# Which queue issues the loads of x and of the softmax, and a planner that counts eight transfers in flight

## The chip, the core and the metric

The kernel runs on one core of a Trainium2 chip. The metric is the device time of one launch in microseconds (us). The core has five engines that run side by side: PE (matrix products), DVE (vector work), ACT (activations and copies), POOL and SP. In this kernel SP issues transfers and does nothing else; POOL issues transfers and does a few small steps at the start. A transfer that SP or POOL issues is moved by the core's 16 DMA engines, and what depends on it waits on a semaphore until it has landed.

## What is computed

Two stages follow each other, over a batch of 8 sequences of 4224 positions with 192 channels. The first is a dynamic convolution: for each position and each of 8 heads, 7 weights pass through a softmax and weigh the last 7 positions of x, 24 channels a head. The second takes that result: a depthwise convolution over 5 positions and a sigmoid make a gate, a matrix product makes a value, and the product of both passes through another matrix.

```python
w = exp(wg - max(wg)); w = w / (sum(w) + 1e-9)            # softmax over 7 taps, per head
y[s, h, :] = sum_k w[s, h, k] * x_pad[s + k, h, :]        # 24 channels a head
gate = sigmoid(sum_k conv_w[k] * y_pad[s + k])            # 5 taps, per channel
out = (gate * (y @ w_val)) @ w_out
```

## The kernel before

**Groups.** The positions are cut into 36 groups of up to 118, counted from 0. A group covers all 8 sequences. Its first step, the *bank*, forms the dynamic convolution as matrix products (L437): 128 small products, whose moving operand is `tb`, a banded matrix of softmax weights, and whose stationary operand is `xt`, a tile of x. So the bank of a group needs 8 loads of `tb` and 8 loads of `xt`. There are two buffers of `tb` and three of `xt`; a load may start once the bank that last used its buffer is done.

**After the bank.** ACT copies the result out of PSUM into `A`, `B` and a scratch `S` (L448, L451, L455). Eight small transfers from `S` fill the holes in `B` (four, L466) and `A` (four, L464); they are called *moves* below. Then come the first tap on ACT (L478), the other taps on DVE (L483), the sigmoid (L488), the value product on PE into `v` (L497 to L504), its product with the gate (L511, L513), the output product into `po` (L524, L531), its copy into `ot` (L546), and two stores of `ot` to the output (L555).

**Softmax.** The softmax of the weights runs ahead of the groups in ten parts (8, 8, 16, then 34 rows a partition, the last 28). A part is loaded into `wt` (L272), worked on by DVE and ACT, spread into `zt` by ACT (L320), and stored to a scratch `zd` in DRAM (L327), from where the loads of `tb` (L424) read it. A part of 34 rows feeds between four and five groups: 16 partitions of 34 rows a sequence are 544 positions.

**Who issues what.** SP issues the loads of `wt` and `tb`, the stores of the output, the first stores of `zd`, and the loads of x of the first and the last group. POOL issues the loads of x of the 34 groups between (L410, 272 transfers), the moves, and the later stores of `zd`. Each queue is served strictly in order: an instruction that waits holds all behind it.

**Eight semaphores a queue kind.** The framework gives the transfers of POOL eight completion semaphores in turn (`DMASW0` to `DMASW7` in the listings below), and those of SP eight others (`DMAHW0` to `DMAHW7`). Before a transfer is issued its engine waits until the last transfer with the same semaphore, the one eight ahead, has landed.

**What sets the order.** A planner, `Order.run`, plays through the whole program with estimated durations. At each step it takes, of the operations whose inputs are ready, the one that can start first on its engine, and breaks near ties by a due time (`key`, in units of groups). The order in which it picks them is the order in which the instructions stand on each engine. It believes that a transfer lands `bytes / RATE` plus `LAND` after the ones before it, with 260 GB/s and 2.8 us for SP and 3.8 us for POOL. It doesn't know of the eight semaphores.

Of the kernel before, what the change touches and what calls it, by code (L numbers as in the profile page):

```python
# [16 lines left out]
class Order:  # L17
# [4 lines left out]
    SWITCH = 0.1  # L22
    SEM = 0.08
    RATE = 260e3
    LAND = {"SP": 2.8, "ACT": 2.8, "POOL": 3.8}

    class Op:
# [14 lines left out]
    def run(self):  # L42
        for o in self.ops:
            o.left = len(o.deps) + len(o.behind)
            for d in o.deps:
                d.users.append((o, True))
            for d in o.behind:
                d.users.append((o, False))
        free, mode, dma = {}, {}, 0.0
        open_ = {}  # L50
        for n, o in enumerate(self.ops):
            if not o.left:
                open_.setdefault(o.eng, []).append((n, o))
        number = {id(o): n for n, o in enumerate(self.ops)}
        done = 0
        while done < len(self.ops):
            best = None
            for eng, c in open_.items():
                if not c:
                    continue  # L60
                t = free.get(eng, 0.0)
                first = min(max(t, o.ready) for _, o in c)
                n, o = min(((n, o) for n, o in c if max(t, o.ready) <= first + self.SLACK), key=lambda x: (x[1].key, x[0]))
                s = max(t, o.ready)
                if best is None or s < best[0]:
                    best = (s, n, o)
            s, n, o = best
            open_[o.eng].remove((n, o))
            e = s + o.dur
            if o.mode is not None:  # L70
                if mode.get(o.eng, o.mode[0]) != o.mode[0]:
                    e += self.SWITCH
                mode[o.eng] = o.mode[-1]
            free[o.eng] = e
            o.start, o.end = s, e + self.SEM
            if o.bytes:
                dma = max(dma, e + 0.8) + o.bytes / self.RATE
                o.end = dma + self.LAND[o.eng]
            o.fn()
            done += 1  # L80
            for u, lands in o.users:
                u.left -= 1
                u.ready = max(u.ready, o.end + u.delay if lands else e)
                if not u.left:
                    open_.setdefault(u.eng, []).append((number[id(u)], u))
        return max(o.end for o in self.ops)
# [3 lines left out]
def tile_dynconv_gated_moe(  # L90
# [9 lines left out]
    nc = tc.nc  # L100

    B, S, D = x.shape
# [3 lines left out]
    P = 128  # L106
# [64 lines left out]
    add = od.add  # L171
# [74 lines left out]
    class Softmax:  # L246
# [34 lines left out]
        def max(self, k):  # L281
            a, b = self.cut[k]
            nc.vector.tensor_reduce(out=self.mx[:, a:b], in_=self.wt[:, a:b], axis=AX.X, op=ALU.max)
# [45 lines left out]
    soft = []  # L329
    zstore = []  # L330

    def softmax(r0, R, k0, k1, early, k2, behind=()):

        s = Softmax(r0, R)
        old = soft[-2]["last"] if len(soft) > 1 else []
        n = s.n * ROW
        b0 = add("DVE", 0.06, early - 1e-3, s.begin, old, behind=behind)
        ld = [add("SP", 0.6, early, lambda: s.load(nc.sync), [b0], bytes=P * n * 4)]
        h = len(s.cut)
        steps = 5 * h + 1 + len(s.zc)  # L340
        done = [0]
# [38 lines left out]
    class Group:  # L380
# [23 lines left out]
        def load_x(self, j):  # L404

            r0 = self.s - FRONT
            if self.whole():
                src = bass.AP(tensor=x.tensor, offset=x.offset + (j * S + r0) * D,
                              ap=[[D, G], [G * D, NGR], [1, D]])
                nc.gpsimd.dma_start(out=self.xb[:, j, 0:D], in_=src)  # L410
            else:
                lo, hi, p = self.rows(j)
                src = bass.AP(tensor=x.tensor, offset=x.offset + (r0 + G * j + lo) * D,
# [180 lines left out]
    for name, cs, w, key in (("c", slice(2 * D, NWT), "DVE", -30), ("v", slice(0, D), "POOL", -29),  # L594
                             ("o", slice(D, 2 * D), "POOL", 1.0)):
        a = lw
# [32 lines left out]
    for m, gp in enumerate(gr):  # L629
        if 2 <= m < len(PARTS) - 1:  # L630
# [4 lines left out]

        old = T[m - 3]["bank"] if m >= 3 else [*xpad, xz]
        late = (() if m == 0 else T[m - 1]["loadt"]) if m < 3 else ()
        d["loadx"] = [add("POOL" if gp.whole() else "SP", 0.55, (-90, -35, -1)[m] if m < 3 else m - 2.2,
                          lambda gp=gp, j=j: gp.load_x(j), old, bytes=G * B * D * 4, behind=late)
                      for j in (range(B) if gp.whole() else gp.chunks)]  # L640
        use = [o for a, sts in rows if a < gp.s + n for o in sts] + [front]
# [86 lines left out]
```

## Time and profile before

| | |
|---|---|
| median of 3 runs | 588.81 us (587.95 to 588.96) |
| the profiled execution | 587.95 us, of which the profile's span is 586.2 us |
| mean granted clock of PE | 0.932 |
| PE busy | 484.9 us, 83% of the span |
| DVE busy | 438.5 us, 75% |
| ACT busy | 345.0 us, 59% |
| POOL busy | 330.2 us, 56% |
| moved by the DMA engines | 123.17 MB, 210 GB/s over the span |

POOL's busy time holds its transfer issues, each about half a microsecond; SP's issues count as no engine's busy time, and its view is a list of issues in order of time. The gap between the median and the span, 2.6 us, lies outside what the profile covers or is scatter between runs.

### The profile page before, as it was taken

To read this page: it belongs to the slowest core of one execution; us is meant where nothing else is said; L and a number is where in the kernel's file an instruction comes from. 1 tells how busy PE (TensorE), PEld (TensorE's weight loads), DVE (VectorE), ACT (ScalarE), POOL (GpSimd) and SP (SyncE) were. 2 spreads that over 40 slices of the span, in tenths; PEclk is the share of its full clock that TensorE was granted. 3 is DMA by queue.
4 is the path that set the end of the run, shared out by engine and by line. 5 is a ranking of instruction groups with operands and counts; after the bars stand their busy time and mean duration, and the time that the engine had idled before them with its cause. 6 is when DMAs were issued, how large, how long until landed. Compare 5 with 4: busy or idle time off the path is not lost.

```text
span 586.2 us, 15839 instructions
## 1 busy us (share of the span) xinstructions
PE 484.9 (83%) x6278; PEld 327.0 (56%) x6278; DVE 438.5 (75%) x488; ACT 345.0 (59%) x533; POOL 330.2 (56%) x613
## 2 busy tenths in 40 slices
PE   2033868599848988999979997998999999999994
PEld 1033535386525764566746673765766675767653
DVE  6776396679857299898887889878975679667780
ACT  4435554478535667458666766586585656546641
POOL 9535956256470666657457455677576687522410
PEclk7557879799987999999979998999999999999999
DMA  5989689738799998879997989799789868775222
GB/s 156 213 239 242 144 223 257 200 99 236 216 236 228 283 266 243 207 207 246 290 259 187 267 217 275 212 261 252 194 217 259 248 158 200 205 183 164 66 60 89
DMA packets 105869, 123.17 MB, mean 210 GB/s; under 512 B 17938, under 2 KB 95615, under 8 KB 103107
## 3 DMA queue, kind: packets, MB, share of 16 engines
q1 hardware_dynamic: 79779, 65.40, 42.5%
q0 software_dynamic: 26016, 56.75, 36.1%
q8 instruction: 50, 0.82, 0.6%
q14 instruction: 24, 0.20, 0.1%
HBM read 64.55 MB, written 51.43 MB: 198 GB/s over the span
## 4 chain that ended last, share of the span: by engine, by line
PE 40%; DMA 30%; POOL 13%; issue 8%; ACT 4%; DVE 2%; SPq 1%; POOLq 0%; ACTq 0%; DVEq 0%
DMA zd<-zt 13%; PE po L524 10%; PE pa L437 10%; POOL xt L410 7%; DMA A<-S 6%; PE po L531 5%; DMA xt<-in_x_dram 5%; PE v L501 5%; DMA tb<-zd 3%; PE v L499 3%; PE v L504 3%; PE v L497 3%; POOL A L464 2%; DMA raw_c<-cd 1%; POOL B L466 1%
## 5 line engine op out<-in xcount | busy, mean ns | idle before, releaser
L483 DVE SCALAR_TENSOR_TENSOR aA<-A,wf,aA 128x944 f32<-128x944 f32 (+1 forms) x144 | 171.6, 1192 | 26.6 <-ACT aA L478 22.8
L437 PE MATMUL pa<-tb,xt 128*32 128x122 f32 (+1 forms) x4608 | 140.5, 276 | 48.8 <-DMA tb<-zd 43.1
L410 POOL DMA_DIRECT2D xt<-in_x_dram x272 | 143.8, 549 | 44.0 <-DMA A<-S 8.7
L437 PEld LDWEIGHTS pa<-tb,xt 128*32 128x32 f32 x4608 | 127.7, 110 | 64.0 <-issue 56.1
L483 DVE SCALAR_TENSOR_TENSOR aB<-B,wf,aB 128x472 f32<-128x472 f32 (+1 forms) x144 | 101.2, 703 | 46.2 <-ACT aB L478 39.0
L466 POOL DMA_DIRECT2D B<-S x144 | 74.7, 525 | 95.8 <-ACT B L451 83.5
L524 PE MATMUL po<-wf,aA 128*118 128x192 f32 (+1 forms) x576 | 117.2, 349 | 11.8 <-DVE aA L511 9.4
L524 PEld LDWEIGHTS po<-wf,aA 128*118 128x118 f32 (+1 forms) x576 | 94.6, 188 | 43.2 <-issue 20.1
L464 POOL DMA_DIRECT2D A<-S x144 | 74.2, 521 | 69.2 <-DMA zd<-zt 36.9
L546 ACT COPY ot<-po 118x768 f32<-118x768 f32 (+1 forms) x72 | 57.8, 803 | 82.3 <-PE po L531 49.4
L531 PE MATMUL po<-wf,aB 64*118 64x192 f32 (+1 forms) x576 | 68.6, 358 | 26.6 <-ACT ot L546 16.8
L531 PEld LDWEIGHTS po<-wf,aB 64*118 64x118 f32 (+1 forms) x576 | 45.8, 183 | 42.6 <-ACT ot L546 18.9
L501 PE MATMUL v<-A,wva 128*128 128x472 f32 (+1 forms) x144 | 63.6, 562 | 0.0
L455 ACT COPY S<-pa 64x488 f32<-64x488 f32 (+1 forms) x72 | 40.5, 562 | 31.1 <-PE pa L437 30.6
L488 ACT ACTIVATE aA<-aA 128x944 f32<-128x944 f32 (+1 forms) x36 | 35.5, 986 | 32.5 <-DVE aA L483 32.5
L511 DVE TENSOR_TENSOR aA<-v,aA 128x944 f32<-128x944 f32 (+1 forms) x36 | 40.7, 1130 | 13.7 <-PE v L504 8.1
L320 ACT COPY zt<-wt 128x192 f32<-128x192 f32 (+3 forms) x100 | 39.1, 461 | 17.5 <-DVE wt L308 11.4
L478 ACT ACTIVATE aA<-A,wf 128x944 f32<-128x944 f32 (+1 forms) x36 | 38.9, 1081 | 14.2 <-DMA A<-S 14.2
L501 PEld LDWEIGHTS v<-A,wva 128*128 128x128 f32 x144 | 27.7, 192 | 31.0 <-issue 30.4
L448 ACT COPY A<-pa 128x488 f32<-128x488 f32 (+1 forms) x72 | 40.5, 565 | 6.5 <-PE pa L437 5.3
L497 PE MATMUL v<-A,wvm 128*64 128x472 f32 (+1 forms) x144 | 38.0, 605 | 7.1 <-DMA A<-S 5.2
L499 PE MATMUL v<-B,wvd 128*128 128x472 f32 (+1 forms) x72 | 39.3, 627 | 0.0
(60 smaller groups left out, 367.5 us busy)
## 6 DMA issues: line engine op xcount, KB each, us to landing
xt<-in_x_dram POOLq DMA_DIRECT2D x272, 96.0 KB, 4.2
tb<-zd SPq DMA_DIRECT2D x285, 88.0 KB
out_dram<-ot SPq DMA_DIRECT2D x35, 672.0 KB
zd<-zt POOLq DMA_DIRECT2D x14, 1104.0 KB, 8.1
wt<-in_weight_gen_dram SPq DMA_DIRECT2D x6, 1120.0 KB
zd<-zt POOLq DMA_DIRECT2D x6, 920.0 KB, 7.5
A<-S POOLq DMA_DIRECT2D x140, 30.5 KB, 4.4
B<-S POOLq DMA_DIRECT2D x140, 15.2 KB, 4.8
```

The source lines that it names most:

```text
L410: nc.gpsimd.dma_start(out=self.xb[:, j, 0:D], in_=src)
L437: nc.tensor.matmul(out=pa[Q * c:Q * c + Q, w * j:w * j + w], lhsT=self.xb[:, u * HB + j, C * h:C * h + Q], rhs=self.t[:, u * HB + j, PAD / ...
L464: nc.gpsimd.dma_start(out=self.A[q:q + n], in_=self.S[p:p + n])
L466: nc.gpsimd.dma_start(out=self.B[HD * u + q:HD * u + q + n], in_=self.S[p:p + n, w * u:w * u + w])
L483: nc.vector.scalar_tensor_tensor(out=a, in0=self.part(g, j), scalar=cw[:, g, j:j + 1], in1=a, op0=ALU.mult, op1=ALU.add)
L497: nc.tensor.matmul(out=v2[HD * u:HD * u + HD, 0:n], lhsT=wvm, rhs=A[u], start=True, stop=False, tile_position=(0, HD * u))
L499: nc.tensor.matmul(out=v2[:, 0:n], lhsT=wvd, rhs=Bt, start=False, stop=True)
L501: nc.tensor.matmul(out=v01[:, u, 0:n], lhsT=wva, rhs=A[u], start=True, stop=False)
L511: nc.vector.tensor_tensor(out=a, in0=self.v01[:, :, 0:n], in1=a, op=ALU.mult)
L524: nc.tensor.matmul(out=po[0:n, u, D * t:D * t + D], lhsT=self.aA[:, c:c + n], rhs=woa, start=first and t == 0, stop=not first, skip_group_ ...
L531: nc.tensor.matmul(out=po[0:n, u, D * t:D * t + D], lhsT=self.aB[hs, c:c + n], rhs=wob[hs], start=first and t == 0, stop=not first, skip_g ...
L546: nc.scalar.copy(out=self.ot[0:n, :, 2 * k:2 * k + 2, :].rearrange("p u t d -> p u (t d)"), in_=self.po[0:n, :, 0:2 * D])
```

## The change

Three things change. The loads of x of the 34 middle groups are issued by SP instead of POOL, and the planner's price for one such issue goes from 0.55 to 0.5 us. The loads of `wt` of the softmax's parts from the fifth on are issued by POOL instead of SP (six parts, eight transfers, since the last part has three). And the planner now knows the eight semaphores: it keeps a list of landing times for POOL and one shared by SP and ACT, and an operation that moves bytes can't start before the one eight ahead on its list has landed, by the planner's own estimate.

```diff
+    LANES = 8
     LAND = {"SP": 2.8, "ACT": 2.8, "POOL": 3.8}
...
         free, mode, dma = {}, {}, 0.0
+        lanes = {"SP": [], "POOL": []}
+        lanes["ACT"] = lanes["SP"]
+
+        def lane(o):
+
+            c = lanes[o.eng] if o.bytes else ()
+            return c[-self.LANES] if len(c) >= self.LANES else 0.0
+
...
-                first = min(max(t, o.ready) for _, o in c)
-                n, o = min(((n, o) for n, o in c if max(t, o.ready) <= first + self.SLACK), key=lambda x: (x[1].key, x[0]))
-                s = max(t, o.ready)
+                at = [(max(t, o.ready, lane(o)), n, o) for n, o in c]
+                first = min(a[0] for a in at)
+                s, n, o = min((a for a in at if a[0] <= first + self.SLACK), key=lambda x: (x[2].key, x[1]))
...
                 o.end = dma + self.LAND[o.eng]
+                lanes[o.eng].append(o.end)
...
-        ld = [add("SP", 0.6, early, lambda: s.load(nc.sync), [b0], bytes=P * n * 4)]
+        q = QUEUES[0 if len(soft) < 4 else 2]
+        ld = [add(q[0], 0.6, early, lambda e=q[1]: s.load(e), [b0], bytes=P * n * 4)]
...
-                nc.gpsimd.dma_start(out=self.xb[:, j, 0:D], in_=src)
+                nc.sync.dma_start(out=self.xb[:, j, 0:D], in_=src)
...
-        d["loadx"] = [add("POOL" if gp.whole() else "SP", 0.55, (-90, -35, -1)[m] if m < 3 else m - 2.2,
+        d["loadx"] = [add("SP", 0.5, (-90, -35, -1)[m] if m < 3 else m - 2.2,
```

Since the planner's rules and prices change, the order changes on every engine. The lists below name, for each instruction, its line, its operation, what it writes and reads, and the shape; the lines of the changed program are about ten higher for the same statement.

POOL, early in the program, before: two stores of `zd`, the moves of group 2, and the loads of x that stand around them. The semaphores that each waits for are in brackets.

```order
L410 DMA xt1_81<-in_x_dram 128x1x192 [waits DMASW4_49,PE_49]
L327 DMA zd_79<-zt0_77 16x8x2208 [waits DMASW5_49,Activation_49]
L327 DMA zd_79<-zt1_78 16x8x2208 [waits DMASW6_49,Activation_49]
L466 DMA B_571<-S_548 8x488 [waits DMASW7_49,Activation_49]
L466 DMA B_571<-S_548 8x488 [waits DMASW0_49]
L466 DMA B_571<-S_548 8x488 [waits DMASW1_49]
L466 DMA B_571<-S_548 8x488 [waits DMASW2_49]
L464 DMA A_592<-S_548 8x976 [waits DMASW3_49,Activation_49]
L464 DMA A_592<-S_548 8x976 [waits DMASW4_49]
L464 DMA A_592<-S_548 8x976 [waits DMASW5_49]
L464 DMA A_592<-S_548 8x976 [waits DMASW6_49]
L410 DMA xt2_82<-in_x_dram 128x1x192 [waits DMASW7_49,PE_49]
```

The same place in the changed program: the stores of the same softmax part and the moves of groups 1 and 2.

```order
L337 DMA zd_79<-zt0_77 16x8x2208 [waits DMASW2_49,Activation_49]
L475 DMA A_446<-S_427 8x976 [waits DMASW3_49,Activation_49]
L475 DMA A_446<-S_427 8x976 [waits DMASW4_49]
L475 DMA A_446<-S_427 8x976 [waits DMASW5_49]
L475 DMA A_446<-S_427 8x976 [waits DMASW6_49]
L337 DMA zd_79<-zt1_78 16x8x2208 [waits DMASW7_49,Activation_49]
L337 DMA zd_79<-zt0_77 16x8x1840 [waits DMASW0_49,Activation_49]
L477 DMA B_611<-S_598 8x488 [waits DMASW1_49,Activation_49]
L477 DMA B_611<-S_598 8x488 [waits DMASW2_49]
L477 DMA B_611<-S_598 8x488 [waits DMASW3_49]
```

Before, the third and the fourth move into `A` wait on `DMASW5` and `DMASW6`, the semaphores of the two stores that stand just ahead of the same group's moves. Now no load of x stands between, one store stands between the moves of group 1, and the semaphore of a store comes up again among the moves of the next group.

SP, some groups later, before: loads of `tb` and stores of the output, without x.

```order
L424 DMA tb_75<-zd 16x8x176 x8
L424 DMA tb_76<-zd 16x8x176 x4
L555 DMA out_dram<-ot 112x8x192
L555 DMA out_dram<-ot 6x8x192
L424 DMA tb_76<-zd 16x8x176 x4
L272 DMA wt<-in_weight_gen_dram 128x1x2240
L424 DMA tb_75<-zd 16x8x176 x3
```

SP, the changed program in its regular stretch.

```order
L435 DMA tb_75<-zd 16x8x176 x8
L421 DMA xt_82<-in_x_dram 128x1x192 x8
L566 DMA out_dram<-ot 112x8x192
L566 DMA out_dram<-ot 6x8x192
L435 DMA tb_76<-zd 16x8x176 x8
L421 DMA xt_80<-in_x_dram 128x1x192 x8
L566 DMA out_dram<-ot 112x8x192
L566 DMA out_dram<-ot 6x8x192
```

A group now has 18 transfers on SP where it had ten, and the loads of the next group's x stand between the loads of this group's `tb` and the stores.

SP at the start of the changed program: the loads of `tb` for group 0, the x of group 1, and then its `tb`.

```order
L435 DMA tb_75<-zd 16x8x176 x6
L282 DMA wt<-in_weight_gen_dram 128x1x2240
L337 DMA zd<-zt_78 16x8x1472
L435 DMA tb_75<-zd 16x8x176
L421 DMA xt_81<-in_x_dram 128x1x192 x8
L435 DMA tb_76<-zd 16x8x176
```

Before, those eight loads of x stood on POOL, on a queue of their own beside SP's loads of `tb`; now SP issues them after the last `tb` of group 0.

## The prediction

> **What bounds the kernel now.** I first cut the span into five stretches with the view of busy time by window (after each engine's busy time comes the number of instructions, then the granted clock, the share of the 16 DMA engines and the rate), then took the same view of the bank's line alone.
>
> ```profile
> core 0: us, PE busy (x) PEld busy (x) DVE busy (x) ACT busy (x) POOL busy (x), PEclk, DMA share, GB/s
> 0.00:60.00 60.00, 14.30 (x270) 11.71 (x270) 41.83 (x56) 27.69 (x50) 36.21 (x55) 0.66 0.86 212
> 60.00:160.00 100.00, 80.45 (x1024) 53.82 (x1025) 75.14 (x83) 60.45 (x92) 56.20 (x104) 0.91 0.73 195
> 160.00:400.00 240.00, 214.40 (x2782) 143.56 (x2780) 191.10 (x207) 154.77 (x238) 145.65 (x280) 0.96 0.90 243
> 400.00:560.00 160.00, 158.12 (x2104) 106.76 (x2105) 119.96 (x133) 94.54 (x147) 92.11 (x177) 1.00 0.73 191
> ...
> 60.00:160.00 100.00, 23.03 (x768) 20.85 (x768) 0.91 0.73 195
> 160.00:400.00 240.00, 62.24 (x2048) 55.91 (x2048) 0.96 0.90 243
> 400.00:560.00 160.00, 44.98 (x1536) 41.09 (x1536) 1.00 0.73 191
> ```
>
> A bank has 128 products, so the three long stretches hold 6, 16 and 12 banks: 16.7, 15.0 and 13.3 us a group. PE stands idle for 45.7 us of the first stretch, 19.6 of the second, 25.6 of the third and 1.9 of the fourth. The fourth is bound by PE. Two banks there show the pace when nothing is waited for:
>
> ```profile
> 435.20 3.75 PE L437 MATMUL pa<-tb,xt 128*32 128x122 f32 x128
> 448.06 3.75 PE L437 MATMUL pa<-tb,xt 128*32 128x122 f32 x128
> ```
>
> That is 12.9 us a group. The other stretches are held up by something else. The chain that ended last names it, over the whole span:
>
> ```profile
> PE 40%; DMA 30%; POOL 13%; issue 8%; ACT 4%; DVE 2%; SPq 1%; POOLq 0%; ACTq 0%; DVEq 0%
> ```
>
> Transfers and POOL together are 43% of the chain. POOL's list in order of time shows how, at the place that the first two listings of the change stand for:
>
> ```profile
> 71.75 4.22 POOL L410 DMA_DIRECT2D xt<-in_x_dram  x8
> 76.39 1.08 POOL L327 DMA_DIRECT2D zd<-zt  x2 [0.42 <-DMA xt<-in_x_dram]
> 77.49 2.08 POOL L466 DMA_DIRECT2D B<-S  x4
> 79.56 1.03 POOL L464 DMA_DIRECT2D A<-S  x2
> 83.59 0.52 POOL L464 DMA_DIRECT2D A<-S  x1 [3.00 <-DMA zd<-zt]
> 89.02 0.52 POOL L464 DMA_DIRECT2D A<-S  x1 [4.91 <-DMA zd<-zt]
> ```
>
> The last two moves of group 2 have their data, but wait until the two stores eight ahead have landed. The chain of waits runs through it: the store, the move, then the first tap that needs `A`.
>
> ```profile
> 76.93 11.81 DMA zd<-zt
> 88.74 0.28 issue
> 89.02 6.28 DMA A<-S
> 95.32 0.04 ACTq L478
> 95.36 0.05 issue
> 95.40 1.09 ACT aA L478
> ```
>
> In the third stretch the waits of POOL's moves into `A` are these (us in total, times, longest):
>
> ```profile
> POOL A L464 <- DMA zd<-zt: 21.3, 8, 7.4
> POOL A L464 <- DMA xt<-in_x_dram: 10.0, 6, 3.7
> POOL A L464 <- DMA B<-S: 7.8, 2, 5.0
> ```
>
> **The change, part by part.** *POOL's queue.* It loses 272 issues, and gains eight.
>
> ```profile
> L410 POOL DMA_DIRECT2D xt<-in_x_dram x272 | 143.8, 549 | 44.0 <-DMA A<-S 8.7
> xt<-in_x_dram POOLq DMA_DIRECT2D x272, 96.0 KB, 4.2
> zd<-zt POOLq DMA_DIRECT2D x14, 1104.0 KB, 8.1
> ```
>
> Eight loads of x are 4.4 us of issue a group; the eight softmax loads, at the 549 ns of such an issue, are 4.4 us in all. What matters more is the count: with only eight moves a group, a store of `zd` has until the next group's moves to land, and 8.1 us is shorter than the 12.9 of a group. At 76 us the fourth move would go right behind the first two, at 79.56 + 1.03 + 0.52 = 81.1 instead of 89.02: 7.9 us. The same happens at 147 us:
>
> ```profile
> 147.25 1.09 POOL L327 DMA_DIRECT2D zd<-zt  x2 [3.82 <-issue]
> 154.52 0.52 POOL L464 DMA_DIRECT2D A<-S  x1 [3.02 <-DMA zd<-zt]
> 159.21 0.52 POOL L464 DMA_DIRECT2D A<-S  x1 [4.16 <-DMA B<-S]
> ```
>
> with 3.0 + 4.2 = 7.2 us. Both are 15.1 of the 19.6 us that PE is idle in that stretch. What is late next is DVE, 75.1 busy of 100, and SP's longer list. The gain lies between 0 (the banks wait for SP instead) and 15.1; I take 9, nearer the waits that are seen, since the DMA engines have room there (share 0.73).
>
> In the third stretch PE's idle 25.6 us is less than the 39.1 that the moves wait, so part of that was covered. The floor is set elsewhere: 0.90 of 240 us is 216 us of work for the DMA engines, against 16 x 12.9 = 206 for PE and 191 for DVE. So the gain can't pass 24 us while the bytes cost what they do. The fullest 40 us show how near the engines come:
>
> ```profile
> 160.00:200.00 40.00, 29.39 (x357) 20.33 (x356) 22.02 (x24) 20.22 (x35) 19.78 (x39) 0.87 0.94 251
> ```
>
> At 0.94 the work takes 216 / 0.94 = 230 us: 10 us gained. I take that, with 0 and 24 as ends.
>
> *The price of the bytes on the other queue.*
>
> ```profile
> q1 hardware_dynamic: 79779, 65.40, 42.5%
> q0 software_dynamic: 26016, 56.75, 36.1%
> ```
>
> SP's queue (q1) moves 65.40 / 42.5 = 1.54 MB for each percent of the engines' span, POOL's 56.75 / 36.1 = 1.57. The x (272 x 96 KB = 26.7 MB) costs 17.4% there instead of 17.0%, 2 us over the kernel, 1 us in the third stretch, which leaves 9 of the 10.
>
> The Trainium skill says in "DMA: Bandwidth & Descriptors", section "Issuing engines are not separate DMA queues", that transfers run on the same 16 engines whoever issues them, and that a second issuer saves only the sequencer's time. The two rates agree with that within 2%; taken alone it gives the second rival below.
>
> *SP's queue.* It gets eight more a group. A quiet group and a crowded one:
>
> ```profile
> 506.72 5.04 SPq L424 DMA_DIRECT2D tb<-zd  x8
> 511.86 1.03 SPq L555 DMA_DIRECT2D out_dram<-ot  x2
> 522.93 4.46 SPq L415 DMA_DIRECT2D xt<-in_x_dram  x7
> ...
> 269.32 4.16 SPq L424 DMA_DIRECT2D tb<-zd  x3
> 273.57 1.25 SPq L555 DMA_DIRECT2D out_dram<-ot  x2
> 274.87 4.27 SPq L424 DMA_DIRECT2D tb<-zd  x5
> ```
>
> Quiet, 18 transfers take 5.04 + 8 x 0.64 + 1.03 = 11.2 us, under the 12.9 of PE. Crowded, the ten took 9.7 instead of 6.1, 3.6 us more: SP itself is held while earlier transfers drain. If that surplus stays per group, 18 take 14.8; if it grows with the count, 18 x 0.97 = 17.5, over the 15.0 that a group takes now. Behind a late SP stand the next loads of `tb`, and then the bank. I take the first, which costs nothing against 15.0 but leaves no room; in the fourth stretch, where 11.2 stands against 12.9 and a surplus may appear, I take 2 us of loss for its 12 groups, between 0 and 12 x (14.8 - 13.3) = 18.
>
> *The start.* PE's first bank waits for `tb`:
>
> ```profile
> PE pa L437 <- DMA tb<-zd: 43.1, 3, 33.6
> 20.00:40.00 20.00, 1.29 (x28) 1.32 (x32) 15.64 (x30) 4.85 (x13) 7.65 (x10) 0.50 0.92 219
> ```
>
> The engines are nearly full there (0.92), and x of group 1, 8 x 96 KB = 786 KB, now goes behind the `tb` of group 0: 786 / 219 = 3.6 us earlier for the first bank. Group 1 needs both and gains less. I take 2, between 0 and 3.6.
>
> *The order as such.* Every engine's list is redrawn, with the same work on it. A misplaced instruction costs a single wait of the kind that the view of waits has as its longest; for PE on ACT this is 7.8:
>
> ```profile
> PE po L531 <- ACT ot L546: 16.8, 6, 7.8
> ```
>
> I take 0, with 8 us either way.
>
> The sum: 2 + 9 + 9 - 2 = 18 us gained. The profiled execution took 587.95 us (span 586.2 and 1.75 around it), which gives 570; the median of the runs is 0.9 higher, so the forecast is **571 us**.
>
> **The rivals.** *SP becomes the bound (slower).* If the surplus grows part of the way with the count, a group of the third stretch takes SP midway between 14.8 and 17.5, 16.2 us: 16 x (16.2 - 15.0) = 19 us lost there, 12 x 0.5 = 6 in the fourth, against 2 + 9 gained before: 14 us lost, 603. It decides from a mean issue of 15.0 / 18 = 0.83 us on; the quiet rows give 0.62, the crowded ones 0.97. Against it: when SP is slow the engines have less to drain, and the surplus shrinks. The Trainium skill ("DMA: Bandwidth & Descriptors", "Queues, rings and completion order") has each DMA engine take the queues in turn, packet by packet. The rows of the two queues give mean packets of 2.2 KB on POOL's and 0.8 KB on SP's, so by that rule SP's loads of `tb` and x would come off worse while a store of `zd` or a load of `wt` is under way, which speaks for this rival.
>
> *The bytes are the bound anyway (no change).* The third stretch is at 0.90; POOL's waits on landings would be the engines' queue seen from the issuer, and the freed issues would only wait elsewhere. Then the third stretch gains nothing, and what the second gains is bytes moved early, given back in the third: 589 less 0 to 2, 588. Against it: in the second stretch the share is only 0.73.
>
> *The waits were nearly all (faster than forecast).* Both ends are reached: 3.6 + 15.1 + 24 = 43, 546 us.
>
> *The planner still believes too much (half the gain).* The rule of eight now matches what the listings show each transfer waiting for, but the planner prices a load of x on SP at 0.5 us, where SP took this for the loads of x that it already issues (min, median, max in ns):
>
> ```profile
> L415 SPq DMA_DIRECT2D xt<-in_x_dram x15: 563/598/876, 3.6 to 526.8; - x15
> ```
>
> By its prices (0.65 for `tb`, 0.5 for x, 0.55 for a store) a group's 18 take 10.3 us, not 11.2 to 14.8. What depends on them then stands too early in the lists and waits, and half of the 18 remains: 580.
>
> **Chances.** Forecast 0.40, the half gain 0.15, the large gain 0.13, the bytes 0.09, SP as the bound 0.23. The likeliest one's own range is 560 to 580. The range must leave out no more than 0.2: I let go most of the large gain's far end and the upper half of SP's case, and keep the rest: **551 to 600**. A measurement of this kernel tells about 0.2% (1.2 us) from no change. Faster has the first three and 0.02 of the bytes' case, 0.70; the same 0.06; slower 0.24.
>
> **What would show it.** Right: no wait of a move on a store of `zd` or on x over a few us; the third stretch at 14.4 us a group with the DMA share at 0.93 or more; the chain with less POOL and more PE; SP's issues at a mean under 0.8 us; the first bank at 35 to 37 us. Wrong: banks that wait on `tb` or xt after the start, SP's issues of `tb` and x stretched beyond 0.83 us, or the fourth stretch slower than 13.3 us a group, all three of SP's case; a third stretch still at 15.0 us with POOL's waits gone, of the bytes'.

## The result, and the profile after

The changed kernel takes 613.11 us (median of 4, 611.97 to 614.59) against 588.38 us (587.70 to 588.96) for the kernel before on the same chip: a ratio of 1.042 (95% interval 1.040 to 1.045). It is 25 us slower, where 18 us of gain had been predicted. Times in this document are medians of all executions of a kernel, while ratios leave out an execution that took over 1.5% longer than the fastest of the same kernel, so the two need not divide out exactly.

The stretches of the changed kernel, in the view by window, for all engines and below for the bank's line alone (now L448):

```profile
0.00:60.00 60.00, 18.75 (x250) 13.35 (x250) 44.07 (x62) 30.32 (x51) 34.42 (x46) 0.66 0.85 210
60.00:160.00 100.00, 79.01 (x1057) 54.39 (x1057) 82.51 (x86) 63.00 (x94) 27.18 (x54) 0.91 0.80 222
160.00:400.00 240.00, 195.97 (x2378) 131.25 (x2380) 177.14 (x190) 135.86 (x218) 65.39 (x130) 0.92 0.80 223
400.00:560.00 160.00, 157.20 (x2162) 107.67 (x2152) 109.04 (x120) 90.88 (x138) 51.76 (x104) 1.00 0.71 188
...
60.00:160.00 100.00, 25.02 (x800) 22.96 (x800) 0.91 0.80 222
160.00:400.00 240.00, 53.70 (x1740) 49.24 (x1744) 0.92 0.80 223
400.00:560.00 160.00, 47.41 (x1599) 42.86 (x1588) 1.00 0.71 188
```

With 128 products a bank these are 6.25, 13.6 and 12.5 banks: 16.0, 17.6 and 12.8 us a group, where it was 16.7, 15.0 and 13.3. The second and the fourth stretch are better than before. The whole loss is in the third, and there the DMA engines have fallen from 0.90 to 0.80: they are not what is short.

The chain's shares after:

```profile
PE 60%; DMA 10%; ACT 8%; DVE 7%; SPq 7%; issue 5%; POOL 2%; ACTq 0%; DVEq 0%; POOLq 0%
```

Transfers and POOL have gone from 43% to 12%. POOL now has time to spare, as its longest entry in the view of waits shows (total, times, longest): the moves wait for their data, and stores of `zd` or loads of x no longer hold them.

```profile
POOL B L477 <- ACT B L462: 304.9, 36, 20.7
```

SP, at two places of its timeline in the changed kernel, one while stores of `zd` and loads of `wt` are under way on POOL's queue, one in the fourth stretch:

```profile
106.00 5.67 SPq L435 DMA_DIRECT2D tb<-zd  x7
111.71 11.36 SPq L421 DMA_DIRECT2D xt<-in_x_dram  x8
123.17 7.03 SPq L566 DMA_DIRECT2D out_dram<-ot  x2
...
412.35 5.10 SPq L421 DMA_DIRECT2D xt<-in_x_dram  x8
417.54 3.27 SPq L435 DMA_DIRECT2D tb<-zd  x4
```

The same eight loads of x take 11.36 us at the one place and 5.10 at the other, both issued without a pause. This reading suggested SP as the cause, but it is only a part of the story.

A finer cut says where the time went. I took the start of the first, the ninth, the seventeenth and the last bank from the timeline's rows of the bank's line. The last two columns are not measurements: they are the times at which the planner (`Order.run`) itself believes that these banks start, read from its list.

| us between starts of banks | before | after | planned, before | planned, after |
|---|---|---|---|---|
| span's start to bank 0 | 38.7 | 35.4 | 36 | 37 |
| bank 0 to 8 | 150.4 | 130.7 | 123 | 128 |
| bank 8 to 16 | 102.3 | 158.8 | 103 | 155 |
| bank 16 to 35 | 260.8 | 252.1 | 248 | 250 |
| planner's total | | | 548 | 608 |

At bank 8 the changed kernel is 23 us ahead (3.3 + 19.7). In the next eight groups it loses 56.5, and it wins 8.7 back in the rest. The planner had planned that loss: 155 us instead of 103 for these eight groups.

### The profile page after: what moved, and what is told of

Its sections match the earlier page's. It is cut to its first block, busy times and chain, and to the rows that moved or that the text cites. A ratio compares the mean times of both kernels' runs of the same rounds, so it can differ in the third digit from the quotient of the medians.

```text
span 611.0 us, 15563 instructions
## 1 busy us (share of the span) xinstructions
PE 493.4 (81%) x6278; PEld 334.7 (55%) x6278; DVE 441.6 (72%) x488; ACT 341.7 (56%) x531; POOL 186.7 (31%) x349
## 4 chain that ended last, share of the span: by engine, by line
PE 60%; DMA 10%; ACT 8%; DVE 7%; SPq 7%; issue 5%; POOL 2%; ACTq 0%; DVEq 0%; POOLq 0%
PE po L535 17%; PE pa L448 15%; PE po L542 8%; PE v L512 7%; PE v L510 5%; PE v L508 4%; PE v L515 4%; SPq L435 4%; DMA xt<-in_x_dram 3%; DMA tb<-zd 3%; SPq L421 3%; DVE aA L494 3%; DMA wt<-in_weight_gen_dram 2%; ACT ot L557 2%; ACT zt L330 1%
## 5 line engine op out<-in xcount | busy, mean ns | idle before, releaser
L448 PE MATMUL pa<-tb,xt 128*32 128x122 f32 (+1 forms) x4608 | 143.7, 281 | 57.9 <-DMA xt<-in_x_dram 41.3
L448 PEld LDWEIGHTS pa<-tb,xt 128*32 128x32 f32 x4608 | 131.5, 113 | 76.2 <-issue 63.3
L477 POOL DMA_DIRECT2D B<-S x144 | 72.4, 509 | 305.1 <-ACT B L462 304.9
L535 PE MATMUL po<-wf,aA 128*118 128x192 f32 (+1 forms) x576 | 121.6, 358 | 18.0 <-ACT ot L557 9.8
L535 PEld LDWEIGHTS po<-wf,aA 128*118 128x118 f32 (+1 forms) x576 | 98.2, 194 | 44.5 <-issue 14.4
L475 POOL DMA_DIRECT2D A<-S x144 | 71.9, 506 | 32.7 <-ACT A L459 13.7
L330 ACT COPY zt<-wt 128x192 f32<-128x192 f32 (+3 forms) x100 | 38.8, 458 | 16.1 <-DVE wt L318 13.3
L524 DVE TENSOR_TENSOR aB<-v,aB 128x472 f32<-128x472 f32 (+1 forms) x36 | 23.1, 642 | 30.1 <-ACT aB L499 15.6
```

Source lines behind the costliest of these rows:

```text
L330: nc.scalar.copy(out=dst, in_=src)
L448: nc.tensor.matmul(out=pa[Q * c:Q * c + Q, w * j:w * j + w], lhsT=self.xb[:, u * HB + j, C * h:C * h + Q], rhs=self.t[:, u * HB + j, PAD / ...
L475: nc.gpsimd.dma_start(out=self.A[q:q + n], in_=self.S[p:p + n])
L477: nc.gpsimd.dma_start(out=self.B[HD * u + q:HD * u + q + n], in_=self.S[p:p + n, w * u:w * u + w])
L535: nc.tensor.matmul(out=po[0:n, u, D * t:D * t + D], lhsT=self.aA[:, c:c + n], rhs=woa, start=first and t == 0, stop=not first, skip_group_ ...
```

## The experiments

In all kernels the three edits are named **x** (the loads of x on SP), **w** (the later loads of `wt` on POOL) and **the rule** (eight transfers in flight in the planner). Times are medians, ratios are against the kernel before on the same chip with 95% intervals. "Planned" is the total that the planner returns.

### One edit at a time, planned anew

x alone:

```diff
-                nc.gpsimd.dma_start(out=self.xb[:, j, 0:D], in_=src)
+                nc.sync.dma_start(out=self.xb[:, j, 0:D], in_=src)
...
-        d["loadx"] = [add("POOL" if gp.whole() else "SP", 0.55, (-90, -35, -1)[m] if m < 3 else m - 2.2,
+        d["loadx"] = [add("SP", 0.5, (-90, -35, -1)[m] if m < 3 else m - 2.2,
```

> Of the three edits only the loads of x on SP; the softmax loads stay on SP and the planner doesn't count to eight. If SP's list of 18 and more transfers a group is the cause (theory SP): about the whole loss, 608 to 620 us, the stretch of 160 to 400 us with no waits of moves on zd stores and SP issuing without a pause. If the softmax loads beside the zd stores on POOL's queue are the cause (theory W): within 5 us of 588. If the planner's new rule is (theory L): 575 to 590.

Measured 624.1 us, 1.059 (1.053 to 1.065), planned 555: a little over theory SP's band, and more than the whole loss of the changed kernel, from one of its three edits.

w alone:

```diff
-        ld = [add("SP", 0.6, early, lambda: s.load(nc.sync), [b0], bytes=P * n * 4)]
+        q = QUEUES[0 if len(soft) < 4 else 2]
+        ld = [add(q[0], 0.6, early, lambda e=q[1]: s.load(e), [b0], bytes=P * n * 4)]
```

> Only the softmax loads from the fifth part on move to POOL; x stays on POOL. Theory SP: 585 to 592, since SP loses six loads and keeps its ten a group. Theory W: slower, 600 or more, with loads of tb that take 2 us of issue while a zd store and a softmax load stand on POOL's queue together. Theory L: 585 to 592.

Measured 596.9 us, 1.010 (1.007 to 1.014), planned 555: a small loss of its own, between the bands of the theories.

The rule alone (the diff of `run` shown with the change):

> Only the planner counts to eight; every transfer stays on its queue. Theory SP and theory W: not slower than 588, and faster (575 to 586) if the waits of moves on zd stores (36.9 us before) are planned away. Theory L: slower, 600 or more, since the order alone does it.

Measured 652.7 us, 1.106 (1.100 to 1.113), planned 659. The rule by itself, with every transfer on the queue that it had, costs the most of all.

x and the rule, without w:

> The change without the move of the softmax loads: x on SP, the planner counts to eight, wt on SP. Theory SP: 608 to 625, as slow as the change or slower, since SP has six more loads. Theory W: within 8 us of 588. Theory L: as slow as the change, 605 to 615.

Measured 623.8 us, 1.058 (1.052 to 1.063), planned 613: as with x alone.

x and w, without the rule:

> Loads of x on SP and the later loads of wt on POOL as in the changed kernel, but the planner without the rule of eight. Orders differ on every engine. Theory Q (SP's issues alone set the loss, about 35 to 42 us, as in the kernels with x on SP in the planner's and in the old order): 615 to 632 us, so the rule, where x is on SP, costs nothing or helps. Theory O (the rule's order costs 20 us or more on top): 585 to 600 us.

Measured 629.2 us, 1.069 (1.060 to 1.079), planned 557.

So x costs 35 us, the rule 63, and all three together 25. They do not add up: where x is on SP, the rule costs nothing (624.1 and 623.8) or helps (629.2 without it, 613.1 with it).

The kernel with the rule alone shows what such a plan does on the chip. From its view of waits and from SP's timeline:

```profile
SPq L565 <- ACT ot L556: 220.8, 25, 21.7
```

```profile
317.42 24.67 SPq L565 DMA_DIRECT2D out_dram<-ot  x6
342.19 15.29 SPq L434 DMA_DIRECT2D tb<-zd  x16
357.57 1.03 SPq L565 DMA_DIRECT2D out_dram<-ot  x2
```

Six output stores stand in a row, each pair waiting for its `ot`, and the sixteen loads of `tb` for the next two banks stand behind them. SP's waits for `ot` are 220.8 us in all here, against 71.2 in the kernel before. The banks of that kernel come in bunches with gaps of 31 to 46 us between (by the bank's rows in the timeline). They are in the plan: from bank 16 on the planner's list has four long gaps of 38, 45, 32 and 51 us, where the chip has 37, 41, 31 and 46.

### The queue and the order apart

Every edit redraws the order of all engines, so these kernels keep one order and change only the engine that issues, at the point where the instruction is emitted. The planner sees nothing of it.

The order of the changed kernel, with x issued by POOL:

```diff
-                nc.sync.dma_start(out=self.xb[:, j, 0:D], in_=src)
+                nc.gpsimd.dma_start(out=self.xb[:, j, 0:D], in_=src)
```

> The order of the changed kernel is kept on every engine, as the planner picks it; only the 272 loads of x of the middle groups are issued by POOL, at the place in the order at which SP issued them. Theory Q (SP's serial issue is the loss: 18 transfers a group at a mean of 0.83 to 0.94 us between 160 and 320 us): SP is back to ten a group, so the third stretch falls from 17.6 us a group to 15.5 or less and the kernel takes 575 to 595 us. Theory O (the redrawn order is the loss, whoever issues): 605 us or more, the third stretch stays above 17 us a group. Theory M (POOL's moves are held behind x again): between, 595 to 605, with POOL's moves waiting on landings of x or zd for over 50 us in all.

Measured 625.7 us (616.5 to 628.2), 1.056 (1.047 to 1.066). Theory O holds, theory Q falls: with x off SP the order is no faster, and its third stretch takes 17.1 us a group (14 banks in 240 us). POOL's moves wait 31 us in all for landings of `zd` and x, less than the 50 that theory M named.

The order of the kernel before, with x issued by SP (the same line, the other way round):

> The order of the kernel before is kept on every engine; only the 272 loads of x are issued by SP instead of POOL, each at its place in the order. Theory Q: SP gets the 18 transfers a group without any other move, and the time rises to 605 to 630 us, with a mean SP issue above 0.83 us between 160 and 320 us. Theory O: 580 to 592 us, since the order is the one that took 588.

Measured 630.6 us, 1.075 (1.069 to 1.080): 43 us for the queue alone. Here theory Q holds in its time, at the upper end of its band, but not in its mark: the mean issue between 160 and 320 us is 0.79 us, not above 0.83. Its stretches, and the waits of its banks:

```profile
60.00:160.00 100.00, 74.42 (x962) 51.86 (x961) 76.56 (x82) 59.05 (x89) 32.40 (x57) 0.86 0.76 209
160.00:400.00 240.00, 198.91 (x2502) 135.95 (x2500) 173.68 (x187) 137.73 (x212) 64.69 (x126) 0.91 0.81 215
400.00:560.00 160.00, 143.85 (x1900) 98.36 (x1898) 107.76 (x121) 89.16 (x139) 44.53 (x88) 0.96 0.72 193
```

```profile
PE pa L437 <- DMA tb<-zd: 51.2, 9, 16.3
PE pa L437 <- DMA xt<-in_x_dram: 50.3, 5, 31.7
```

Its third stretch takes 16.8 us a group (240 us for 1824 products of the bank, 14.25 banks). SP issues 261 transfers there at a mean of 0.80 us, 209 of 240 us.

The order of the changed kernel, with half of x on each queue:

```diff
-                nc.sync.dma_start(out=self.xb[:, j, 0:D], in_=src)
+                (nc.sync if j < 4 else nc.gpsimd).dma_start(out=self.xb[:, j, 0:D], in_=src)
```

> The order of the changed kernel is kept on every engine; four of the eight loads of x of a group are issued by POOL, so SP has 14 transfers a group. Theory O (in the changed kernel the stretched order sets the pace of the third stretch, SP only follows): the long gaps between banks stay, 603 to 618 us. Theory Q (SP sets it): 14 x 0.85 = 11.9 us a group, and 585 to 600 us.

Measured 608.5 us, 1.032 (1.026 to 1.037). SP's issues now take 168 of the 240 us instead of 212, and the time falls by 5 us only. The same place in the timeline of PE, first in the changed kernel, then in this one:

```profile
297.70 1.06 PE L515 MATMUL v<-B,wvb 64*128 64x472 f32 x4
304.49 1.64 PE L542 MATMUL po<-wf,aB 64*118 64x192 f32 x8 [5.72 <-DVE aB L524]
306.73 2.91 PE L535 MATMUL po<-wf,aA 128*118 128x192 f32 x8 [0.60 <-DVE aA L522]
...
315.54 3.79 PE L448 MATMUL pa<-tb,xt 128*32 128x122 f32 x128
```

```profile
296.11 1.06 PE L515 MATMUL v<-B,wvb 64*128 64x472 f32 x4
302.91 1.63 PE L542 MATMUL po<-wf,aB 64*118 64x192 f32 x8 [5.73 <-DVE aB L524]
305.15 2.91 PE L535 MATMUL po<-wf,aA 128*118 128x192 f32 x8 [0.60 <-DVE aA L522]
...
313.87 3.77 PE L448 MATMUL pa<-tb,xt 128*32 128x122 f32 x128
```

The two agree to two hundredths of a microsecond, 1.6 to 1.7 us apart. PE waits 5.7 us for DVE's product `aB`, and the bank stands behind it in PE's list, with the output product and the next `v` between. The bank waits for no load here: it waits for its place. From bank 8 to 16 this kernel takes 156.1 us, the one with x on POOL 159.9, the changed kernel 158.8.

One bank is one place; the whole stretch from bank 8 to 16 says the same. These are its rows in the view by window in the kernel before, in the changed one and in this one, and then waits of PE in this one:

```profile
189.10:291.40 102.30, 95.48 (x1350) 65.04 (x1349) 81.95 (x88) 67.69 (x104) 64.22 (x123) 1.00 0.91 247
166.10:324.90 158.80, 119.77 (x1409) 81.78 (x1410) 118.54 (x127) 90.38 (x145) 40.87 (x81) 0.89 0.82 230
167.10:323.20 156.10, 119.13 (x1411) 79.94 (x1409) 119.12 (x127) 90.79 (x145) 58.61 (x114) 0.90 0.81 227
```

```profile
PE po L542 <- DVE aB L524: 14.9, 5, 5.7
PE po L535 <- ACT ot L557: 5.5, 6, 1.1
...
PE pa L448 <- DMA xt<-in_x_dram: 1.5, 1, 1.5
```

The new order lets DVE do 127 instructions, 119 us, between these eight banks, where it did 88, 82 us, before. PE is idle for 37 us there (before 7), and only 1.5 us of that end with a load that a bank needs. The granted clock is lower there too (0.90 against 1.00); what that adds, no run separates.

The order of the kernel before, with half of x on each queue:

> The order of the kernel before is kept on every engine; four of the eight loads of x of a group are issued by SP, four by POOL. SP has 14 transfers a group. Theory Q with a threshold (SP's issues bind only where 14 or 18 of them pass a group's 12.9 to 15 us): 14 x 0.8 = 11.2 us, 584 to 597 us. A cost in proportion to the transfers moved: half of the 42 us of the same order with all eight on SP, 604 to 612 us.

Measured 594.4 us, 1.005 (1.000 to 1.009). Four loads more on SP cost at most 1%, eight cost 7.5%: a threshold and not a price per transfer.

The order of the kernel before, x on SP, and the output stores issued by POOL:

```diff
-            nc.sync.dma_start(out=dst, in_=self.ot[lo:hi].rearrange("p u t d -> p (u t) d"))
+            nc.gpsimd.dma_start(out=dst, in_=self.ot[lo:hi].rearrange("p u t d -> p (u t) d"))
```

> The order of the kernel before is kept; all loads of x are issued by SP and the two stores of the output of each group by POOL. SP has 16 transfers a group and never waits for ot. Theory Q: against the 631 us of the same order with 18 on SP it gains 2 x 0.8 x 34 = 54 us of SP's issuing, of which half lies on the path, and the 39 us of waits for ot: 595 to 612 us. If the loss is not SP's issuing but the bytes on its queue: 622 us or more, since the bytes of x stay there. A third way: the stores that wait for ot hold POOL's moves, over 630 us.

Measured 614.7 us, 1.044 (1.037 to 1.052). It gains 16 of the 43 us and just misses theory Q's band. SP issues 245 transfers in the third stretch, at a mean of 0.85: 209 of 240 us, as much as with the stores on it. POOL now waits 31.6 us for `ot` ahead of the moves, the third way that was named; its share of the time is not separated.

The order of the changed kernel, with the later loads of `wt` issued by SP:

```diff
-        ld = [add(q[0], 0.6, early, lambda e=q[1]: s.load(e), [b0], bytes=P * n * 4)]
+        ld = [add(q[0], 0.6, early, lambda: s.load(nc.sync), [b0], bytes=P * n * 4)]
```

> The order of the changed kernel is kept; the loads of wt from the fifth part on are issued by SP again, eight transfers in all, so only stores of zd and the moves are left on POOL's queue. Theory P: half of the large packets leave the other queue, and the time falls by 5 to 12 us, to 601 to 608. Theory D: the same bytes pass through the same engines, 610 to 617 us. Theory Q alone: eight issues more on SP, 613 to 620 us.

Measured 612.5 us, 1.041 (1.034 to 1.048), the changed kernel's time, in theory D's band: w does nothing in this order.

### What stretches an issue of SP

The order of the changed kernel, the large transfers of POOL's queue cut into four:

```diff
-                part(0, HP, B, 0, n)
+                for i in range(4 if eng is nc.gpsimd else 1):
+                    k = 4 if eng is nc.gpsimd else 1
+                    part(0, HP, B, n * i // k, n * (i + 1) // k)
...
+        def pieces(self, c, z, eng):
+            a, e = self.zc[c]
+            for lo in range(0, e - a, 3):
...
```

> The order of the changed kernel is kept; each store of zd and each load of wt on POOL's queue is cut into four (rows of about 2.2 KB instead of 8.8 KB a partition), so POOL issues four times as many of these and the bytes stay. Theory P (SP's small packets come off worse because each of POOL's packets is large, and SP's issues are stretched by that): the mean SP issue between 160 and 320 us falls from 0.88 to 0.75 us or less and the kernel to 585 to 603 us. Theory D (SP is held because all 16 DMA engines are full, whatever the packets' size): 608 to 618 us and the mean issue within 0.05 us of the changed kernel's.

Measured 608.4 us (602.5 to 610.7), 1.034 (1.028 to 1.041). This is the lower edge of theory D's band, and D's mark is met: the mean issue between 160 and 320 us is 0.86, where the changed kernel has 0.88.

The order of the kernel before with x on SP, each load of x with half the channels, and then with half the partitions (in both, the tiles of x are cleared at the start, and the half of x that is not loaded is missing from the result):

```diff
-                              ap=[[D, G], [G * D, NGR], [1, D]])
-                nc.sync.dma_start(out=self.xb[:, j, 0:D], in_=src)
+                              ap=[[D, G], [G * D, NGR], [1, D // 2]])
+                nc.sync.dma_start(out=self.xb[:, j, 0:D // 2], in_=src)
```

> The order of the kernel before with all x on SP, but each load of x takes only the first 96 of the 192 channels (the rest of the tile stays zero, so the second half of the channels is left out of the result): half the bytes, the same 128 rows a load. If SP's issues are stretched because its queue drains by bytes: the mean issue falls to 0.70 us or less and the time from 631 to 590 to 605 us. If it is a price per row or per issue: 620 us or more, mean issue as before at 0.8.

```diff
-                              ap=[[D, G], [G * D, NGR], [1, D]])
-                nc.sync.dma_start(out=self.xb[:, j, 0:D], in_=src)
+                              ap=[[D, G // 2], [G * D, NGR], [1, D]])
+                nc.sync.dma_start(out=self.xb[0:P // 2, j, 0:D], in_=src)
```

> As the run before, but each load of x takes only the first 64 of 128 partitions with all channels (the other positions are left out): half the bytes and half the rows a load. By bytes or by rows: 590 to 605 us with a mean issue of 0.70 us or less. A fixed price per issue: 620 us or more. If this run gains and the one with half-width rows doesn't, it is the number of rows.

Measured 625.8 us (1.064, 1.059 to 1.070) and 612.0 us (1.038, 1.033 to 1.043) against 630.6 with whole loads. Half the bytes gain 5 us, half the rows 19. The third stretch of the two:

```profile
160.00:400.00 240.00, 196.74 (x2464) 133.62 (x2460) 176.07 (x190) 138.77 (x215) 65.88 (x128) 0.93 0.75 192
```

```profile
160.00:400.00 240.00, 207.06 (x2606) 140.07 (x2608) 180.31 (x195) 142.39 (x220) 65.89 (x128) 0.93 0.73 200
```

The DMA engines are at 0.75 and 0.73 over the stretch, and SP still issues for 213 and 214 of the 240 us, at a mean of 0.80 and 0.79 us against 0.80 with whole loads. So neither the bytes of x nor the engines' mean load is what holds SP. The 19 us of half the rows do not come from shorter issues; what gave them back stays open.

What the slow issues have in common is seen when SP's issues of the third stretch are sorted by whether a store of `zd` or a load of `wt` had been issued, by any engine, in the 10 us before (count and mean, from the trace's issues):

| third stretch | near | else | SP issuing |
|---|---|---|---|
| before | 96 at 1.05 us | 78 at 0.66 | 153 of 240 us |
| after | 90 at 1.15 | 170 at 0.64 | 212 |
| before's order, x on SP | 124 at 0.97 | 137 at 0.64 | 209 |
| the same, half the channels | 121 at 1.00 | 147 at 0.63 | 213 |
| the same, half the partitions | 124 at 0.98 | 148 at 0.62 | 214 |
| after's order, large ones cut | 109 at 1.03 | 147 at 0.64 | 206 |

Away from these transfers an issue takes 0.62 to 0.66 us in these six kernels. Near them it takes 0.97 to 1.15, with ten transfers a group as with eighteen. The price goes with the softmax's 1.1 MB transfers and changes little with the size of the transfers that pay it. Nearness alone is not enough, and a mean over the stretch hides the rest. Sorted once more by the DMA share of the microseconds in which each issue stands, in the changed kernel 65 issues near such a transfer at a share of 0.80 or more took 1.34 us in the mean, 25 near one at a lower share 0.66, and 38 away from one at the high share 0.73. With half the channels these are 1.26, 0.71 and 0.68. The long issues stand where both come together. The Trainium skill has, in "DMA: Bandwidth & Descriptors", section "Queues, rings and completion order", each DMA engine switch between rings packet by packet; the size of the large transfers' rows moved the mean from 1.15 to 1.03 and the kernel by 5 us, so that rule can account for a small part here. Why an issue is held there stays open: neither run with smaller loads of x removed it.

### Both causes weakened

The rule alone, counting sixteen ahead instead of eight:

```diff
-    LANES = 8
+    LANES = 16
```

> The kernel before with the rule alone, but counting a transfer as held until the one sixteen ahead has landed, so that the rule hardly ever binds in the plan; queues as before. The planner's own total (the return value of its run) is 553 us here, 659 with the rule at eight and 548 without it. Theory O (the plan itself was stretched by the rule, because by the planner's landing times eight in flight are too few, and the chip follows the order): 580 to 600 us, against 653 with eight. If the rule's loss came from the rule's changed choice among ready operations and not from its landing times: 620 us or more.

Measured 590.7 us, 1.004 (1.000 to 1.008), planned 553: 62 of the rule's 63 us are gone.

The changed kernel with four of the eight loads of x on POOL, planned so, and the rule at sixteen:

```diff
-    LANES = 8
+    LANES = 16
...
-                nc.sync.dma_start(out=self.xb[:, j, 0:D], in_=src)
+                (nc.sync if j < 4 else nc.gpsimd).dma_start(out=self.xb[:, j, 0:D], in_=src)
...
-        d["loadx"] = [add("SP", 0.5, (-90, -35, -1)[m] if m < 3 else m - 2.2,
+        d["loadx"] = [add("POOL" if gp.whole() and j >= 4 else "SP", 0.5, (-90, -35, -1)[m] if m < 3 else m - 2.2,
```

> The changed kernel, planned anew, with both suspects weakened: four of the eight loads of x of a group are issued by POOL, and the rule counts sixteen ahead. If the two together are the loss: 583 to 598 us, near the kernel before. If something else in the change (the loads of wt on POOL) holds the kernel: over 603 us.

Measured **584.7 us, 0.991 (0.988 to 0.995)**, planned 553: 0.9% faster than the kernel before. Its stretches:

```profile
60.00:160.00 100.00, 86.27 (x1062) 57.68 (x1062) 90.37 (x97) 71.31 (x109) 48.77 (x94) 0.95 0.84 231
160.00:400.00 240.00, 207.97 (x2746) 143.46 (x2746) 186.08 (x202) 149.93 (x233) 108.29 (x207) 0.94 0.86 242
400.00:560.00 160.00, 159.06 (x2107) 106.63 (x2107) 117.48 (x128) 92.33 (x137) 68.24 (x132) 1.00 0.68 171
```

The DMA share is 0.84 and 0.86 in the second and third stretch; in the kernel before it was 0.73 and 0.90. Bank 8 starts at 176.7 us, 12 earlier than before; banks 8 to 16 take 117.9, 16 more; banks 16 to 35 take 255.0, 6 less.

Which of its edits it needs, by undoing one: w undone, and the rule taken out.

```diff
-        q = QUEUES[0 if len(soft) < 4 else 2]
+        q = QUEUES[0]
```

> The kernel with half of x on SP and the rule at sixteen (585 us), planned anew with the later loads of wt back on SP. If the gain comes from the split of x: 580 to 588 us. If the loads of wt on POOL are needed for it (SP's list is clear of loads whose rows are 9 KB a partition): 589 to 597 us.

Measured 597.8 us, 1.015 (1.012 to 1.018), planned 559.

```diff
-            c = lanes[o.eng] if o.bytes else ()
+            c = ()
```

> The same with half of x on SP and the later loads of wt on POOL, but the planner without any rule on transfers in flight. If the split of x and the place of the loads of wt make the gain and a loose rule matters little: 580 to 590 us. If the rule at sixteen is what spaces the order: 592 to 605 us.

Measured 589.5 us, 1.000 (0.997 to 1.003), planned 564. The last one lies in the band of a rule that matters little, yet the gain over the kernel before is gone with it. So the loads of `wt` on POOL are needed here and worth 13 us, where alone w cost 6 (1.010), and the loose rule is worth 5. Since all three kernels have orders of their own, these numbers are those of plans and not of single instructions.

## Why the prediction was wrong, point by point

**What bounds the kernel before.** The reading of the waits held, their price is not shown. The start gained 3.3 us (predicted 2, bound 3.6), with the first bank at 35.4, inside the 35 to 37 named. Banks 0 to 8 gained 19.7, where 9 had been taken and 15.1 was the bound for the stretch up to 160 us. Two runs say that this is not POOL's queue alone: with x on SP in the order of before, the moves' waits on stores fall from 36.9 to 5.9 us and banks 0 to 8 take 147.9, only 2.5 less; with x on POOL in the new order they take 140.4, already 10.0 less. So about half of the gain came with the order while x was still on POOL, and the order had been put at nothing.

**The fourth stretch.** A loss of 2 us was forecast, and 13.3 became 12.8 us a group. SP's mean issue is 0.65 us there, near the 0.62 of the quiet rows.

**The third stretch, the step that failed first.** The forecast was "10 us gained. I take that, with 0 and 24 as ends", for 14.4 us a group. It came to 17.6. The bounds were made of POOL's waits, the DMA share and the pace of PE, and all of these take for granted that the new order lets the work use the freed time. It did not, which is the next step.

**"The order as such ... I take 0, with 8 us either way."** This is the wrong term. The order cost the changed kernel its result: with half of x taken from SP, and with all of it, the eight groups from bank 8 on keep taking 156 to 160 us, against 102 in the order before. The bound of 8 us was a single wait's length, as if the planner might misplace one instruction. But the change gave the planner a new constraint, and its own plan became 60 us longer (608 instead of 548). The chip followed it: 659 planned and 653 measured for the rule alone, 553 and 591 once it counted sixteen. The order is not the only thing that can hold this kernel: without the rule, but with x and w, it takes 629.2 us, and SP issues for 205 of the third stretch's 240 us. Either cause is enough by itself; with both weakened the time falls to 584.7.

How the plan becomes so long can be read from the planner's numbers. Between banks 8 and 16 it has SP wait 72 us for the transfer eight ahead, because it believes that a transfer lands 8.1 us after its issue begins, in the mean. On the chip, by the semaphore events of the trace, SP's transfers of these eight groups landed 5.0 us after their issue began, in the mean, and half of them within 3.6. The changed kernel's view of waits has SP held by landings for little (its two largest entries on landings, over the whole kernel):

```profile
SPq L421 <- DMA tb<-zd: 7.4, 6, 2.1
SPq L435 <- DMA xt<-in_x_dram: 7.0, 5, 2.7
```

So the rule is true to the semaphores, but the landing times that it is fed are over half as long again as the chip's, and eight are then too few. That sixteen repair it is shown; that shorter landing times with eight would do the same was not tried.

**"I take the first, which costs nothing against 15.0 but leaves no room."** SP's term has the right size and the wrong price. The mean issue of the third stretch came to 0.82 us, and 18 of them to 14.7, next to the 14.8 taken. In the order of before, though, this cost 43 us and not nothing. There the mean was 0.80, 14.4 a group, and a group took 16.8: SP also waits for `ot` and for its turn, so it held the kernel though it issued for only 87% of the time (209 of 240 us). With 14 transfers SP was at 76% (228 at a mean of 0.80, 184 us), and the loss was at most 1%. In the changed kernel's own order, which is slow anyway, SP's share of the loss is only the 5 us that half of x gave back. My two cases for the surplus, "per group" or "with the count", were both beside it: the surplus goes with the time near a transfer of the softmax while the engines are full. The prediction reads a long issue as SP held "while earlier transfers drain"; the runs show when an issue is long, and not what holds it.

**The rivals.** *SP becomes the bound* had the sign, and 603 against 613 is close, but for most of it the cause was another. Its mechanism is shown in the order of before, where it sets in below the 0.83 us that I gave as its point. *The bytes are the bound* falls: the share went down to 0.80, and the kernel of 585 us has 0.86. *The planner still believes too much* is half turned around: of landings it now believes too little, of SP's issues still too much (0.5 to 0.65 us planned, 0.82 measured; x alone was planned at 555 us and took 624). *The waits were nearly all* fits banks 0 to 8 in size, and only these.

**The signs that were named.** Moves that no longer wait and a first bank at 35 us came true and told nothing of the sum. A mean SP issue under 0.8 was to mean right; it was 0.86 and 0.82 in the middle stretches, and the listed mark of SP's case showed too, banks that wait for loads after the start (the first row's longest is the start itself):

```profile
PE pa L448 <- DMA xt<-in_x_dram: 41.3, 3, 29.8
PE pa L448 <- DMA tb<-zd: 10.3, 1, 10.3
```

These 22 us (11.5 and 10.3) looked like most of the loss. In the kernel with its order and half of x back on POOL about half of them are left, by the same view:

```profile
PE pa L448 <- DMA xt<-in_x_dram: 11.3, 3, 8.8
```

The half that went is worth at most the 5 us that this kernel gains, and the 20 us that it still loses stand elsewhere in the order. A mark for the order was missing from the list.

## What to carry to other kernels

Where a change touches a planner's rules, its own planned length and planned starts, old and new, come first: a plan that has become 60 us longer is a forecast, and "the order, plus or minus one wait" is no bound for it. It forecasts the order alone, though: x alone was planned at 555 us and took 624, since the plan knew nothing of SP's loaded issue time. A serial issuing queue should be costed at its loaded issue time and taken as full at under nine tenths of the period, since it also waits in order; moving half of the transfers can be free where moving all of them costs 7%. To tell a queue from an order, keep the order and change only the issuer.

## What was not expected of the hardware

SP's issue time depends on what else is in flight and hardly on its own transfer: 0.62 to 0.66 us away from the softmax's 1.1 MB transfers, 0.97 to 1.15 within 10 us behind one (six kernels), the same for loads of half the bytes. The long ones among these stand where the DMA engines are at 0.80 or more. The Trainium skill says in "DMA: Bandwidth & Descriptors", section "Issuing engines are not separate DMA queues", that a second issuer saves only the sequencer's time, usually small beside the transfer. For a single transfer the trace agrees: an issue of SP takes 0.80 us of the 4.6 that pass from its start to the landing, in the mean of the third stretch of the kernel with the order of before and x on SP. But SP issues one transfer after another, and the sum is not small: giving SP all of x instead of half cost 36 us (594.4 and 630.6) in one and the same order.
